# Weight scales found by way of DRAM instead of TensorE, and paced spreading of keys and queries, in a two-branch attention kernel

## The chip, the cores and the metric

The kernel runs on one core of a Trainium2 chip. The metric is the device time of one execution in microseconds. Three executions of the kernel before took 2800.7, 2800.9 and 2802.06 us; the median is 2800.9 us.

## The reference

Two attention blocks A and B read the same input `x` (2048 tokens, 640 features) and have weights of their own; a gate mixes their outputs.

```python
def _A_ref(x, wqkv, wo):                       # _B_ref is the same with its own weights
    H = 32; Dh = D // H                        # 32 heads of 20 features
    qkv = (x @ wqkv).reshape(B, S, 3, H, Dh)   # then q, k, v by head
    scores = einsum("bhqd,bhkd->bhqk", q, k) * Dh ** -0.5
    p = softmax(scores, axis=-1)
    o = einsum("bhqk,bhkd->bhqd", p, v)
    return o.transpose(0, 2, 1, 3).reshape(B, S, D) @ wo
g = sigmoid((x * gate_w).sum(-1, keepdims=True))
return g * a + (1 - g) * b
```

All inputs and the output are float32.

## The kernel before, in words

**Groups, units, steps.** The 64 heads of both blocks are 16 groups of four. A group has four blocks of 512 queries, and each of these has eight steps of 256 keys, so there are 512 steps. In a step TensorE makes eight products of keys and queries (`scores`, L639), ScalarE takes the exponential of each (L642), and two *value products* (`values`, L657; eight TensorE passes each) add the weighted values of the step before. Up to 15 steps ahead of a query block, TensorE makes the scores a second time the other way round (`max_mm`, L581), and VectorE finds their row maxima (L589, L592; for some of them ScalarE makes a helper with L585). Seven PSUM banks go round between the three engines (`take` and `give`).

**Block work.** Projections of the next group (`project_a`, `project_r`, `project_v`) and output products (`out_tiles`) are cut into blocks, and a step takes up to two of them (`slot`; their matmuls have L382). An output tile first loads its attention output from DRAM (`o_in<-o_scr`, L699), then lets `OWAIT` = 20 turns pass, then asks for its products.

**Turns.** What is not a matmul is written as generators in the list `side`. `advance` lets each of them go one `yield` further, and it is called eight times a step: this is a *turn*. A `yield PRODUCT` parks a generator until a value product is due (`product`, just before `values`), so that its small full-height matmuls stand beside the value product.

**Scales.** All weights are split into two float16 parts after a division by a power of two. For it `scales` (L167) needs the largest absolute value over the 128 partitions: the partition maxima are transposed on TensorE (L173), reduced on VectorE (L177), turned into powers of two by four small VectorE operations (`powers`), put on a diagonal (L183), sent back to all partitions by two TensorE products with ones (L190), and copied from PSUM (L193). Apart from the start, this is done twelve times: for queries and keys three times (`scales_qk`), for values seven times (`scales_v`), and for the output weights twice (`scales_o`). The results feed GpSimd, which splits the weights (L312 to L315).

**Spreading.** `project_a` leaves a group's keys and queries feature by feature. `spread` and `spread_differences` copy them by DMA to the rows where `scores` and `max_mm` want them, one transfer after each `yield` of `rows` (L428, L430), on SyncE's queue (SP). A group has two halves: the first takes 22 transfers (four of them for key differences), the second 18. Both halves wait until the group before has begun (`later`, L490), and then they go side by side. SP's queue is in order: it also issues the weights' loads (L240, L343, L344, L366), the row maxima's way through DRAM (L613, L617), the attention outputs' stores (L763), and the loads and stores of the output tiles (L699, L704, L732).

**What sets the order.** The program order of each engine is made by the loop over `G` (L1112) with the strings `STEP`; within an engine nothing is reordered when it runs. `clock`, `spend` and `tick_block` are the planner's own estimates, which choose PSUM banks.

Of the kernel before, what the change touches and what calls it, by code (L numbers as in the profile page):

```python
# [3 lines left out]

# [7 lines left out]
F32 = mybir.dt.float32  # L12
I32 = mybir.dt.int32
AF = mybir.ActivationFunctionType
OP = mybir.AluOpType
AX = mybir.AxisListType
# [3 lines left out]
P = 128  # L20
# [18 lines left out]
QUARTERS = (0, 128, 256, 384, 512)  # L39
FINE = (2, 3, 5, 6)  # L40
OB = 3
OWAIT = 20
AFROM, ADUE, ADUES = -24, -8, 4
QKMAX = (0, 10, 42, 10)
VEARLY = 338
# [23 lines left out]
def kernel(  # L69
# [10 lines left out]
    nc = tc.nc  # L80
# [5 lines left out]
    wts = ctx.enter_context(tc.tile_pool(name="wts", bufs=2))  # L86
    dram = ctx.enter_context(tc.tile_pool(name="dram", bufs=1, space=DRAM))
# [30 lines left out]
    o_scr = [dram.tile([2, D, S], F16, name=f"o_scr{z}") for z in range(2)]  # L118
    m_scr = [dram.tile([4, 16, P], F16, name=f"m_scr{i}") for i in range(2)]
    y_scr = dram.tile([NT, P, D], F32, name="y_scr")  # L120


    clock = {"pe": 0.0, "done": 0.0, "act": 0.0, "dve": 0.0}
# [11 lines left out]
    def spend(engine, cost, ready=0.0):  # L135

        clock[engine] = max(clock[engine], ready) + cost
        return clock[engine] + T_BACK
# [28 lines left out]
    def scales(maxima, n, then):  # L167

        for _ in range(REST):
            yield  # L170
        yield PRODUCT
        i, pt = take()
        nc.tensor.transpose(pt[:n, :P], maxima[:, :n], ident)  # L173
        tick_block(0.1, free_at[i])
        yield
        e = wts.tile([5, 8], F32, name="e", tag="scl", bufs=2)
        nc.vector.tensor_reduce(e[:n, 0:1], pt[:n, :P], axis=AX.X, op=OP.max)  # L177
        give(i, spend("dve", 0.3, clock["done"]))
        spend("dve", 1.0)
        powers(e.bitcast(I32)[:n, :], 1)  # L180
        dg = wts.tile([5, 2, 5], F32, name="dg", tag="scd", bufs=2)
        for k in range(2):
            nc.vector.tensor_scalar(dg[:n, k, :n], ident[:n, :n], e[:n, 3 + k:4 + k], None, op0=OP.mult)  # L183
        for _ in range(REST):
            yield
        yield PRODUCT
        i, pb = take()
        tick_block(0.1, free_at[i])
        for k in range(2):
            nc.tensor.matmul(pb[:, k * n:(k + 1) * n], ones[:n, :], dg[:n, k, :n], start=True, stop=True)  # L190
        yield
        both = wts.tile([P, 10], F32, name="both", tag="scb", bufs=2)
        nc.vector.tensor_copy(both[:, :2 * n], pb[:, :2 * n])  # L193
        give(i, spend("dve", 0.2, clock["done"]))
        then(both[:, :n], both[:, n:2 * n])

    def set_x(r_x, r, inv):
        nc.vector.tensor_copy(r_x, r)
        nc.vector.tensor_copy(inv_x, inv)

    def set_qk(i, r, inv):
        nc.vector.tensor_copy(r_qk[i], r)
        e = esc[i]
        nc.vector.tensor_tensor(e, inv[:, 0:1], inv_x, op=OP.mult)
        nc.vector.tensor_scalar(e, e, inv[:, 1:2], float(DH ** -0.5 / QKS ** 2), op0=OP.mult, op1=OP.mult)
        nc.vector.tensor_tensor(e, e, inv_x, op=OP.mult)

    def set_v(gg, r, inv):
        nc.vector.tensor_copy(r_v[gg], r)

        f = gg % (NG // 2) * 160
        while f < (gg % (NG // 2) + 1) * 160:
            p0 = f % P
            n = min(P - p0, (gg % (NG // 2) + 1) * 160 - f, (P, 32, 64, 32)[p0 // 32])
            nc.vector.tensor_copy(wrow[gg // (NG // 2)][p0:p0 + n, f // P:f // P + 1], inv[p0:p0 + n])
            f += n

    def scales_qk(i, maxima):

        return scales(maxima, 2, lambda r, inv: set_qk(i, r, inv))  # L220

    def scales_v(gg, maxima):
        return scales(maxima, 1, lambda r, inv: set_v(gg, r, inv))

    def scales_o(z, maxima):
        def then(r, inv):
            nc.vector.tensor_copy(r_o[z], r)
            nc.vector.tensor_scalar(f_o[z], gates[:, z, :], inv, inv_x, op0=OP.mult, op1=OP.mult)
            nc.vector.tensor_scalar(f_o[z], f_o[z], 1.0 / QKS, None, op0=OP.mult)

        return scales(maxima, 1, then)

    def largest(dst, src):
        nc.vector.tensor_reduce(dst, src, axis=AX.XY, op=OP.max,
# [46 lines left out]
    side = []  # L281
# [43 lines left out]
    spread_done = set()  # L325
# [107 lines left out]
    def spread(g, hl, t0, n, q=(0, 1), k=(0, 1), queues=repeat(nc.sync)):  # L433


        cols = slice(t0, t0 + n)
        r0 = 32 * (g % 4)
        qt = QT[g % 2]
        for j in range(2):
            base = 64 * j  # L440
            for pair in k:
                f = slice((2 * pair + j) * DH, (2 * pair + j + 1) * DH)
                yield from rows(KT[g % 2][:, pair, cols], base, 0, hl[f], DH, True, queues)
            if 0 in q:
                f = slice(GF + j * DH, GF + (j + 1) * DH)
                yield from rows(qt[:, 0, cols], base, 0, hl[f], DH, False, queues)
            if 1 in q:
                if j == 0:
                    yield from rows(qt[:, 1, cols], base, 0, hl[GF + 40:P], 8, False, queues)
                f = slice(r0 + 12 * j, r0 + 12 + 20 * j)  # L450
                yield from rows(qt[:, 1, cols], base, 8 * (1 - j), rk[g // 4][f, :, cols], 12 + 8 * j, False, queues)

    def project_r(i, ch):
        n = slice(ch * QB, (ch + 1) * QB)
        yield from project_chunk(blk["r", i], rk[i][:, 0, n], rk[i][:, 1, n], ch, QUARTERS if 4 * i in FINE else THIRDS)
        r_done.add((i, ch))
# [17 lines left out]
    def spread_differences(g, queues=repeat(nc.sync), to=None):  # L474
        dd = differences.pop(g)
        for j in range(2 if g == 0 else 1):
            for pair in range(2):
                f = slice((2 * pair + j) * DH, (2 * pair + j + 1) * DH)
                yield from rows((KD[g % 2] if to is None else to)[:, pair], 64 * j, 0, dd[f], DH, True, queues)

    def project_a(g, ch):
        if ch % 2 == 0:
            half_tiles(g)
        hl = blk["q", g]
        n = slice((ch % 2) * QB, (ch % 2 + 1) * QB)
        yield from project_chunk(blk["a", g], hl[:, 0, n], hl[:, 1, n], ch, QUARTERS if g in FINE else THIRDS)
        if ch == 1:
            key_differences(g, hl, work.tile([P, QB], F32, name="fs"), work.tile([P, 2, QB], F16, name="dd", bufs=1))
        if ch % 2 == 1:
            def later():  # L490
                for _ in range(10):
                    yield
                while not {(g // 4, c) for c in (ch - 1, ch)} <= r_done or now[0] < (g - 1) * NQ * NS + 1:
                    yield
                if ch == 1:
                    yield from spread_differences(g)
                yield from spread(g, hl, ch // 2 * 1024, 1024)
                spread_done.add((g, ch // 2))

            side.append(later())  # L500
# [383 lines left out]
    load, split_next = weights_a(1)  # L884
# [4 lines left out]
    r, inv = found  # L889
# [89 lines left out]
    def at(G, f):  # L979
        todo.setdefault(G, []).append(f)  # L980
# [11 lines left out]
    for g in range(2 * NG):  # L992
        b = g * step
        n = g + 1
        if n < 2 * NG:
            parts = 4 if n in FINE else 3
            fill += [((-8, 15)[g] if g < 2 else b + AFROM, b + ADUE + ADUES * ch if g else 4 + 3 * ch, parts, project_a(n, ch))
                     for ch in range(4)]
            if n + 1 < 2 * NG:
                tasks(b + 2 if g else 9, 3, weights_a(n + 1))  # L1000
            i = g // 4 + 1
            if i < 4:
                if g % 4 == 0:
                    z, c0 = i // 2, 320 * (i % 2)
                    srcs = max_tasks([[(wqkv[z], part * D + c0 + 160 * k) for k in range(2)] for part in range(2)],
                                     lambda m, i=i: scales_qk(i, m))
                    tasks(b + QKMAX[i], 2, srcs)
                if g % 4 == 2:
                    tasks(b + 6, 3, weights_r(i))
                    parts = 4 if 4 * i in FINE else 3  # L1010
                    fill += [(b + 12, b + 22 + 4 * ch, parts, project_r(i, ch)) for ch in range(4)]
            gg = g // 2 + 1
            if gg < NG and g % 2 == 0:
                load, scale, split = weights_v(gg)
                at(max(b - 8, 0), load)
                if gg < NG - 1:
                    at(max(b - 5, 3), lambda scale=scale: side.append(scale()))
                at(max(b - 1, 7), split)
                fill += [(max(b + 2, 10), b + 2 * step - 4 + j // 2, 2, project_v(gg, j)) for j in range(0, NT, 2)]
    early = weights_v(NG - 1)  # L1020
    at(VEARLY, early[0])
# [164 lines left out]
```

## Time and profile before

| | before |
|---|---|
| median of three executions | 2800.9 us |
| the profiled execution | 2800.33 us |
| its span (first to last instruction) | 2798.5 us |
| mean granted TensorE clock | 0.995 |
| TensorE (PE) busy | 2744.9 us |
| ScalarE (ACT) busy | 2524.6 us |
| VectorE (DVE) busy | 2452.3 us |
| GpSimd (POOL) busy | 671.9 us |

The span lies within the profiled execution, so 1.8 us of it are outside. The first value product starts at 105.6 us and the last pass of one at 2781.3 us: the 512 steps take 2675.7 us, 5.23 us each on average, and a turn is an eighth of it, 0.653 us. PEld is TensorE's weight load. A row of the timeline has its start, its length, engine, line, operation, output and inputs, how many instructions are merged into it, and in brackets the idle time ahead of it with what ended it. A row of the stretches' view has the stretch, its length, the busy time of PE, PEld, DVE, ACT and POOL (with counts), then TensorE's granted clock, the mean busy share of the 16 DMA engines, and GB/s. "SPq" is the time in which SP issues a DMA, not the transfer.

### The profile page before, as it was taken

What the parts mean: (1) busy time and instruction counts of PE and PEld (TensorE: products, weight loads), DVE (VectorE), ACT (ScalarE), POOL (GpSimd) and SP (SyncE); (2) the same over time, 40 slices, a digit from 0 to 9 for tenths busy, and PEclk for the clock granted to TensorE, in tenths of its full rate; (3) what the DMA queues carried; (4) which work ended last, traced back from release to release, by engine and by line L of the source; (5) the groups of instructions that cost most, each with busy time, mean ns of one, the idle gap of its engine ahead of it and who ended that gap; (6) DMA issues with size and microseconds to landing.
All of it is one profiled execution on the core that took longest, in us unless ns stands there. A gap on an engine that the chain in (4) does not pass through costs nothing.

```text
span 2798.5 us, 61863 instructions
## 1 busy us (share of the span) xinstructions
PE 2744.9 (98%) x23122; PEld 939.9 (34%) x23122; DVE 2452.3 (88%) x4795; ACT 2524.6 (90%) x5106; POOL 671.9 (24%) x914
## 2 busy tenths in 40 slices
PE   6999999999999999999999999999999999999998
PEld 3433332333333332333333323333333333322222
DVE  6789899889999999888888988989988898999982
ACT  3799999999999999999999889999999999989987
POOL 5322122312222421321221212222342202200111
PEclk9999999999999999999999999999999999999999
DMA  4020102001020211202012231122201112131112
GB/s 136 19 57 14 41 11 46 7 21 25 14 64 17 62 27 54 48 8 61 21 35 70 58 77 31 38 63 54 61 23 42 33 46 63 31 88 55 42 48 75
DMA packets 172943, 124.57 MB, mean 45 GB/s; under 512 B 103264, under 2 KB 142488, under 8 KB 172640
## 3 DMA queue, kind: packets, MB, share of 16 engines
q1 hardware_dynamic: 170096, 118.99, 16.9%
q8 instruction: 181, 2.97, 0.4%
q0 software_dynamic: 1600, 0.96, 0.2%
q14 instruction: 122, 1.00, 0.1%
q10 hardware_dynamic: 944, 0.66, 0.1%
HBM read 54.54 MB, written 31.85 MB: 31 GB/s over the span
## 4 chain that ended last, share of the span: by engine, by line
PE 92%; DVE 3%; ACT 2%; DMA 1%; POOL 1%; issue 1%; SPq 0%; POOLq 0%; ACTq 0%; DVEq 0%
PE acc L657 35%; PE bank L581 19%; PE bank L382 19%; PE bank L639 18%; DVE mpart L592 2%; ACT pt L642 1%; DMA xs<-in_A_x_dram 0%; ACT rl L585 0%; DMA wv<-in_A_wqkv_dram 0%; PE bank L820 0%; DVE rl L589 0%; PE bank L190 0%; SPq L428 0%; DVE ot L743 0%; PE bank L869 0%
## 5 line engine op out<-in xcount | busy, mean ns | idle before, releaser
L642 ACT ACTIVATE pt<-bank 128x512 f32<-128x512 f32 x4096 | 2169.2, 612 | 166.7 <-PE bank L639 101.7
L592 DVE TENSOR_REDUCE mpart<-bank 128x1 f32<-128x512 f32 x2976 | 1865.2, 682 | 222.2 <-PE bank L581 114.8
L657 PE MATMUL acc<-pt,v 128*21 128x512 f32 x8192 | 1082.2, 600 | 0.6 <-DVE ot L743 0.4
L639 PE MATMUL bank<-qt,kt 64*128 64x512 f16 x4096 | 1051.7, 380 | 4.2 <-ACT pt L642 2.0
L581 PE MATMUL bank<-kt,qt 60*128 60x512 f16 x3536 | 1021.3, 380 | 5.1 <-ACT pt L642 1.7
L581 PEld LDWEIGHTS <-qt 60*128 60x128 f16 x4096 | 238.1, 94 | 862.9 <-issue 802.9
L589 DVE CUSTOM_DVE_ANT_0 rl<-bank,rl 128x512 f32<-128x512 f32 x560 | 378.7, 680 | 16.7 <-ACT rl L585 10.6
L585 ACT ACTIVATE rl<-bank 128x512 f32<-128x512 f32 x560 | 329.7, 595 | 10.7 <-PE bank L581 8.7
L639 PEld LDWEIGHTS <-kt 64*128 64x128 f16 x4096 | 235.5, 94 | 238.7 <-issue 122.8
L382 PE MATMUL bank<-xx,wbh 128*128 128x168 f16 (+3 forms) x2400 | 286.0, 239 | 2.6 <-ACT xx L873 1.9
L657 PEld LDWEIGHTS acc<-pt,v 128*21 128x21 f32 x8192 | 143.1, 99 | 428.8 <-issue 421.9
L382 PE MATMUL bank<-xx,wbl 128*128 128x168 f16 (+3 forms) x1200 | 256.1, 237 | 0.0
L751 POOL TENSOR_TENSOR ot<-ot,sq 128x512 f32<-128x512 f32 x63 | 66.0, 1047 | 773.4 <-DVE sq L748 773.4
L382 PEld LDWEIGHTS <-wbh 128*128 128x128 f16 x2400 | 189.4, 98 | 109.5 <-issue 102.0
L581 PE MATMUL bank<-kd,qt 60*128 60x512 f16 x560 | 203.8, 380 | 1.6 <-DMA kd<-dd 1.2
L382 PE MATMUL bank<-woh,o_in 128*128 128x320 f16 (+1 forms) x640 | 156.4, 302 | 5.5 <-DMA o_in<-o_scr 5.4
L411 POOL CAST cq<-fs 128x512 f16<-128x512 f32 x60 | 36.6, 610 | 521.0 <-ACT fs L409 517.4
L382 PE MATMUL bank<-wvh,xx 128*128 128x160 f16 (+1 forms) x1280 | 155.2, 234 | 0.1
L382 PEld LDWEIGHTS <-xx 128*128 128x128 f16 x1920 | 131.5, 97 | 52.3 <-issue 49.1
L382 PE MATMUL bank<-wvl,xx 128*128 128x160 f16 (+1 forms) x640 | 137.3, 231 | 0.5 <-POOL wvl L322 0.5
L382 PEld LDWEIGHTS <-wbl 128*128 128x128 f16 x1200 | 117.4, 98 | 4.3 <-issue 0.8
L382 PEld LDWEIGHTS <-o_in 128*128 128x128 f16 (+1 forms) x960 | 80.9, 97 | 97.7 <-issue 63.8
(131 smaller groups left out, 1259.1 us busy)
## 6 DMA issues: line engine op xcount, KB each, us to landing
y_scr<-y_out SPq DMA_DIRECT2D x48, 320.0 KB
y_out<-y_scr SPq DMA_DIRECT2D x32, 320.0 KB
kt<-cq SPq DMA_DIRECT2D x120, 80.0 KB
o_scr<-on SPq DMA_DIRECT2D x240, 40.0 KB
o_in<-o_scr SPq DMA_DIRECT2D x64, 96.0 KB
kt<-cq SPq DMA_DIRECT2D x136, 40.0 KB
wstage<-in_B_wqkv_dram SPq DMA_DIRECT2D x13, 400.0 KB
xs<-in_A_x_dram SPq DMA_DIRECT2D x8, 640.0 KB
```

The costliest lines, as they stand in the source:

```text
L382: nc.tensor.matmul(out_ap, a, b, start=(k == 0), stop=(k == len(pairs) - 1))
L411: nc.gpsimd.tensor_copy(hi, f)
L581: nc.tensor.matmul(pt, QT[g % 2][r, pair, q0:q0 + P], k, start=True, stop=True)
L585: nc.scalar.activation(relus[u, j], pt, AF.Relu)
L589: nc.vector.tensor_tensor_reduce(rl, pt, rl, 1.0, LOW, OP.add, OP.max, m)
L592: nc.vector.tensor_reduce(m, pt, axis=AX.X, op=OP.max)
L639: nc.tensor.matmul(et, KT[g % 2][r, pair, kt * P:(kt + 1) * P], QT[g % 2][r, pair, qb * QB:(qb + 1) * QB], start=True, stop=True)
L642: nc.scalar.activation(pt, et, AF.Exp, scale=factor(g // 4))
L657: nc.tensor.matmul(acc[32 * h:32 * h + VW, :], V[(g // 2) % 2][:, kt, (g % 2) * GH + h, :], ptiles.pop((G, kk, h)), start=(kt == 0), stop= ...
L751: nc.gpsimd.tensor_tensor(t3, t3, sq.unsqueeze(2).to_broadcast([P, 16, 32]), op=OP.mult)
```

## The change

`scales_qk`, `scales_v` and `scales_o` call a new function, `scales_by_dram`. The partition maxima are stored to DRAM; ten turns later one transfer loads them into every partition (128 x 128 values, or 128 x 128 pairs for queries and keys); 18 turns after that VectorE takes the maximum in every partition at once and goes on with `powers`. No TensorE instruction is left in it, and nothing waits for a value product. The start still uses `scales`. The values' weights are loaded and reduced one step earlier. `paced` puts a further `yield` behind each transfer of a spread (`PACE` = 2; group 1 keeps its old rate), and the second half of a group waits for the first. As the code stands, a transfer comes every second turn. `OWAIT` goes from 20 to 24.

```diff
-OWAIT = 20
+STORED, LOADED = 10, 18
+OWAIT = 24
+PACE = 2
...
+    s_scr = [dram.tile([P * 5], F32, name=f"s_scr{i}") for i in range(3)]
+    scale_turns = counter()
...
+    def scales_by_dram(maxima, n, then):
+
+        turn = next(scale_turns)
+        scr = s_scr[turn % 3].rearrange("(p n) -> p n", n=5)[:, :n]
+        yield
+        yield
+        nc.sync.dma_start(scr, maxima[:, :n])
+        for _ in range(STORED):
+            yield
+        rows = wts.tile([P, P, 2], F32, name="srows", tag="srows", bufs=2)[:, :, :n]
+        nc.sync.dma_start(rows, scr.unsqueeze(0).to_broadcast([P, P, n]))
+        for _ in range(LOADED):
+            yield
+        e = wts.tile([P, 10], F32, name="es", tag="ses", bufs=2)
+        nc.vector.tensor_reduce(e[:, :n], rows.rearrange("p q n -> p n q"), axis=AX.X, op=OP.max)
+        spend("dve", 0.35 * n + 0.5)
+        powers(e.bitcast(I32), n)
+        then(e[:, 3 * n:4 * n], e[:, 4 * n:5 * n])
...
-        return scales(maxima, 2, lambda r, inv: set_qk(i, r, inv))
+        return scales_by_dram(maxima, 2, lambda r, inv: set_qk(i, r, inv))
...
-        return scales(maxima, 1, lambda r, inv: set_v(gg, r, inv))
+        return scales_by_dram(maxima, 1, lambda r, inv: set_v(gg, r, inv))
...
-        return scales(maxima, 1, then)
+        return scales_by_dram(maxima, 1, then)
...
+    def paced(gen, n):
+        for _ in gen:
+            for _ in range(n):
+                yield
...
                 while not {(g // 4, c) for c in (ch - 1, ch)} <= r_done or now[0] < (g - 1) * NQ * NS + 1:
                     yield
+                while ch == 3 and (g, 0) not in spread_done:
+                    yield
+                turns_each = 1 if g == 1 else PACE
                 if ch == 1:
-                    yield from spread_differences(g)
-                yield from spread(g, hl, ch // 2 * 1024, 1024)
+                    yield from paced(spread_differences(g), turns_each)
+                yield from paced(spread(g, hl, ch // 2 * 1024, 1024), turns_each)
                 spread_done.add((g, ch // 2))
...
-                at(max(b - 8, 0), load)
+                at(max(b - 9, 0), load)
                 if gg < NG - 1:
-                    at(max(b - 5, 3), lambda scale=scale: side.append(scale()))
-                at(max(b - 1, 7), split)
+                    at(max(b - 6, 3), lambda scale=scale: side.append(scale()))
+                at(max(b - 1, 8), split)
```

**First place: TensorE at the fifth scale of the values.** Before, the scale's transpose stands ahead of one value product (L657), between scores (L639), maxima (L581) and the matmuls of a block (L382):

```order
L639 MATMUL bank_93<-qt_81,kt_83 128x512
L173 MATMUL bank_89<-ident,m_18933 1x128
L657 MATMUL acc<-pt,v_87 21x512 x4
L581 LDWEIGHTS qt_80
L581 MATMUL bank_94<-kt_82,qt_80 128x512
```

One step further on, the two products with ones stand ahead of the next first value product:

```order
L639 MATMUL bank_92<-qt_81,kt_83 128x512
L190 MATMUL bank_91<-dg,ones 128x1 x2
L657 MATMUL acc<-pt,v_87 21x512 x4
L581 LDWEIGHTS qt_80
L581 MATMUL bank_90<-kt_82,qt_80 128x512
```

Now, with the lines moved by 31, the value product (L688) follows the scores (L670) directly; L612 are the maxima:

```order
L670 MATMUL bank_92<-qt_81,kt_83 128x512
L688 MATMUL acc<-pt,v_87 21x512 x4
L612 LDWEIGHTS qt_80
L612 MATMUL bank_94<-kt_82,qt_80 128x512
```

Three TensorE instructions are gone from each of the twelve scales, one that stood ahead of one value product and two ahead of another, and two PSUM banks fewer are taken each time.

**Second place: SP's queue where the second scale of queries and keys and the fourth of the values come together.** In the program of after, the store of the pair's maxima (L207), the row maxima's way (L644, L648), an output tile's store (L763), the two loads (L211) and the next output tile's loads (L730) stand in this order:

```order
L207 DMA s_scr_128<-m_14307 128x2
L207 DMA s_scr_126<-m_14309 128x1
L644 DMA m_scr_123<-m4r 16x4x32 x4
L648 DMA qt_80<-m_scr_123 4x512 x4
L763 DMA y_scr<-y_out 128x640
L211 DMA srows<-s_scr_128 128x128x2
L211 DMA srows<-s_scr_126 128x128x1
L730 DMA o_in<-o_scr_121 128x3x128 x2
```

The two big loads are neighbours in one queue, behind a store that waits for an output product, and VectorE's two reductions of them (L215) stand nine instructions apart.

**Third place: SP's queue in the spread of group 10.** Before, the load of output tile 6 of the second job (L699) stands behind nearly all of both halves' transfers (L428, L430); these are the rows just ahead of it:

```order
L430 DMA kt_82<-cq 20x1024
L430 DMA qt_80<-rk 20x1024
L613 DMA m_scr_124<-m4r 16x4x32 x4
L428 DMA qt_80<-cq 40x1x1024
L430 DMA qt_80<-cq 20x1024
L428 DMA qt_80<-rk 40x1x1024
L699 DMA o_in<-o_scr_121 128x2x128 x2
L704 DMA y_out<-y_scr 128x640
```

Now the same load (L730) comes where the first half is not yet half done (L451, L453):

```order
L451 DMA qt_80<-cq 40x1x1024
L644 DMA m_scr_124<-m4r 16x4x32 x4
L453 DMA qt_80<-cq 20x1024
L451 DMA qt_80<-cq 16x1x1024
L730 DMA o_in<-o_scr_121 128x2x128 x2
L735 DMA y_out<-y_scr 128x640
L453 DMA qt_80<-cq 8x1024
```

The same output products of that tile follow four steps after its turn in both programs; what changed is how many transfers SP has to issue ahead of its load.

More of the change, by code (lines that the diff above doesn't have):

```diff
@@ L2 @@
 from contextlib import ExitStack
-from itertools import cycle, repeat
+from itertools import count as counter, cycle, repeat
 import concourse.bass as bass
```

## The prediction

> **What bounds the kernel now.** I read the page's busy times first, then the chain that ended last.
>
> ```profile
> PE 2744.9 (98%) x23122; PEld 939.9 (34%) x23122; DVE 2452.3 (88%) x4795; ACT 2524.6 (90%) x5106; POOL 671.9 (24%) x914
> ```
> ```profile
> PE 92%; DVE 3%; ACT 2%; DMA 1%; POOL 1%; issue 1%; SPq 0%; POOLq 0%; ACTq 0%; DVEq 0%
> ```
>
> TensorE is busy 98% of the span and owns 92% of the chain. Time taken from it should come off the end, unless VectorE or ScalarE, at 88% and 90% on average, is full at that very place. TensorE's timeline shows one scale at close range; these are its value products (L657) and the scale's own rows.
>
> ```profile
> 1907.62 1.06 PE L657 MATMUL acc<-pt,v 128*21 128x512 f32 x8
> ...
> 1909.36 0.27 PE L173 MATMUL bank<-ident,m 128*1 128x128 f32 x1
> 1909.56 1.06 PE L657 MATMUL acc<-pt,v 128*21 128x512 f32 x8
> ...
> 1913.06 1.05 PE L657 MATMUL acc<-pt,v 128*21 128x512 f32 x8
> ...
> 1915.22 0.60 PE L190 MATMUL bank<-dg,ones 1*128 1x1 f32 x4 [0.26 <-ACT pt L642]
> 1915.75 1.06 PE L657 MATMUL acc<-pt,v 128*21 128x512 f32 x8
> ...
> 1919.39 1.06 PE L657 MATMUL acc<-pt,v 128*21 128x512 f32 x8
> ...
> 1921.14 1.06 PE L657 MATMUL acc<-pt,v 128*21 128x512 f32 x8
> ```
>
> The distance between value products is a ruler. From 1919.39 to 1921.14 it is 1.75 us, the plain short distance. With the transpose it is 1.94, with the two products 2.69 (1913.06 to 1915.75); 0.26 of that is a wait for a PSUM bank. The long distance, with a block of projections in it, is 3.50 ahead of the products and 3.64 behind them.
>
> **Part 1: twelve scales leave TensorE.** One scale costs 0.19 + 0.94 us here, and up to 0.14 in the block behind it; I take 1.2 us. Their number:
>
> ```profile
> L173 PE MATMUL bank<-ident,m x12: 270/270/271, 128.1 to 1999.5; 128*1 128x128 f32 x9, 128*2 128x128 f32 x3
> ```
>
> Twelve times 1.2 is **14.4 us**, and 15.2 with the whole 0.14. The lower bound comes from VectorE, which is nearly full where no block runs:
>
> ```profile
> 420.00:440.00 20.00, 19.76 (x139) 4.63 (x138) 19.44 (x45) 17.94 (x37) 8.34 (x7) 1.00 0.05 12
> 748.00:766.00 18.00, 17.46 (x117) 4.23 (x110) 17.62 (x41) 15.48 (x31) 4.63 (x4) 1.00 0.07 14
> ...
> 1077.00:1099.00 22.00, 21.28 (x154) 6.38 (x152) 20.76 (x55) 18.51 (x38) 5.30 (x5) 1.00 0.16 42
> ```
>
> It idles 0.6, 0.4 and 1.2 us in these stretches, which hold four scales. If TensorE's 4.8 us come back only that far, 12 us are left of the 14.4. VectorE's own work hardly moves: a reduction over 128 values gives way to another, `powers` stays, three tiny operations go.
>
> **Part 2: the spread stops blocking SP.** One stall stands alone in the trace.
>
> ```profile
> 1644.38 1.06 PE L657 MATMUL acc<-pt,v 128*21 128x512 f32 x8
> ...
> 1647.58 1.06 PE L657 MATMUL acc<-pt,v 128*21 128x512 f32 x8
> ...
> 1649.33 1.06 PE L657 MATMUL acc<-pt,v 128*21 128x512 f32 x8
> ...
> 1656.32 0.45 PE L382 MATMUL bank<-woh,o_in 128*128 128x320 f16 x1 [5.39 <-DMA o_in<-o_scr]
> ...
> 1659.42 1.47 PE L657 MATMUL acc<-pt,v 128*21 128x512 f32 x8
> ...
> 1661.58 0.63 PE L657 MATMUL acc<-pt,v 128*21 128x512 f32 x4
> ```
>
> From 1649.33 to 1659.42 are 10.09 us where the same kind of distance before (1644.38 to 1647.58) is 3.20, and the short one behind is 2.16 instead of 1.75: together **7.3 us**. TensorE waited for `o_in`, which SP issued at 1654.24, late because every transfer of the spread holds SP 0.8 us while two halves hand it one each per turn of 0.65 us:
>
> ```profile
> 1654.24 0.92 SPq L699 DMA_DIRECT2D o_in<-o_scr  x2
> ```
> ```profile
> L428 SPq DMA_DIRECT2D kt<-cq x136: 762/797/1121, 40.5 to 2491.1; - x136
> ```
>
> Now one half comes at a time, a transfer every second turn: SP needs 0.8 of 1.3 us and keeps up, and this load is issued four steps, 21 us, ahead of its use. The price of pacing: a group's last transfer goes out some 9 steps after the group before has begun, instead of 2. The maxima that read it start 17 steps after that beginning at the earliest (15 steps ahead of the group's own), so 8 steps (42 us) cover it, and I cost it at nothing; without that cover every later step would wait. `OWAIT` shifts products by half a step within dues of several steps: nothing, with at most one block's delay either way.
>
> **Part 3: the new wait.** VectorE now waits for a DMA, and behind it in its queue stand all maxima and so the PSUM banks. The load writes 128 x 128 values separately (the tile has two columns, the DRAM rows five), 16384 pieces of 4 or 8 bytes. No row shows such a load alone. The nearest are the four loads of L366, together 4 x 5 x 128 = 2560 pieces of 128 bytes, and a store of L613, 16 x 4 = 64 pieces of 64 bytes, each in a stretch of its own:
>
> ```profile
> 480.52:483.04 2.52, 2.52 (x23) 0.56 (x20) 2.08 (x5) 2.26 (x6) 0.00 (x0) 1.00 0.86 130
> 500.67:500.86 0.19, 0.19 (x5) 0.19 (x4) 0.19 (x1) 0.19 (x2) 0.00 (x0) 1.00 0.23 21
> ```
> ```profile
> q1 hardware_dynamic: 170096, 118.99, 16.9%
> ```
> ```profile
> kd<-dd POOLq DMA_DIRECT2D x8, 20.0 KB, 2.0
> ```
>
> Share times length times 16 engines over pieces gives 0.86 x 2.52 x 16 / 2560 = 13.5 ns for 128 bytes and 10.9 ns for 64. The straight line through both gives an estimate of 8.5 ns at 4 bytes, my value. An engine has 1024 pieces: 8.7 us, and with the 2.0 us that a small transfer takes to land, 10.7. The upper end is the queue's mean packet, 0.169 x 16 x 2798.5 us / 170096 = 44.5 ns (of 700 bytes): 47.6 us.
>
> How long may it take? The reduction comes 18 turns behind the load:
>
> ```profile
> L657 PE MATMUL acc<-pt,v x8192: 592/600/1026, 105.6 to 2781.3; 128*21 128x512 f32 x200
> ```
>
> 2675.7 us over 512 steps of eight turns is 0.653 us a turn, so 11.8 us. SP is often ahead of its turn: it may load as soon as the store has landed, 17 us ahead of the reduction. I take 14.5 in the middle. A load that lands in 10.7 us costs nothing at either end.
>
> The pair is different: two loads, one behind the other, in one queue.
>
> ```profile
> 1075.84 0.15 DVE L276 TENSOR_REDUCE m<-wmax 128x2 f32<-128x8 f32 x1
> ```
> ```profile
> 1084.69 0.35 SPq L732 DMA_DIRECT2D y_scr<-y_out  x1
> ```
>
> The maxima are ready at 1075.8, and the reductions come 30 turns later, at 1095.4. SP cannot load before the output store at 1084.69, so from 1085.0 on; the second load lands 2 + 2 x 8.7 = 19.4 us later, at 1104.4. VectorE waits 9.0 us. TensorE goes on for about 0.9 until its seven banks are taken and loses 0.4 restarting, as above: **8.5 us**. Its lower end is nothing, if SP gets the loads out early.
>
> [...] The 500.67 stretch moved 64 pieces in 0.19 us, 3.0 ns each over all engines. [...]
>
> **The sum.** 2800.33 (the profiled execution: span 2798.5 and 1.8 around it) - 14.4 - 7.3 + 8.5 = 2787.1; the median of the runs lies 0.6 above that execution, so **2787.7 us**.
>
> **The rivals.**
> - *The loads land late* (slower). All ten single loads stall VectorE, and with it TensorE, once a piece costs over 12.2 ns, (14.5 - 2) / 1.024. The gains of 21.7 us are used up at 12.7 ns. At the 13.5 ns of the 128-byte row each single wait is 1.3 us and the pair's 18.7: 13 + 18.7 - 21.7 = +10, 2811 us. At 44.5 ns it would be about 3190. For it: all engines read the same few DRAM rows, which no row here shows. Against it: the price falls with size in both rows.
> - *Pieces go one after another.* 16384 x 8.5 ns = 139 us a load; ten waits of 127 and one of 269: about 4320 us. Against it: 2560 pieces went in 2.52 us. [...]
> - *VectorE paces, or the tile's load stays late* (same). If part 1 gives only 6 us, 2796; if the early `o_in` is caught behind something else and the 7.3 stay, 2795.
> - *The pair doesn't wait*: 2779.
>
> **How the numbers follow.** Forecast 0.55; no wait in the pair 0.15; same 0.13; loads late 0.16; one after another 0.01. A run of this kernel can tell 0.2%, 5.6 us, from no change: faster means below 2795.3. So faster 0.70, same 0.13, slower 0.17. The range takes in the pair without a wait and the cases of no change, 2776 to 2803; the late loads beyond stay out.
>
> **What would show it.** Right: no matmul of the scales behind the start; distances of 1.75 where 1.94 and 2.69 stood; no distance of 10 us near 1650; VectorE waiting for `srows` once, near 1095, for 9 us, and landing of a single load within 11 us of its issue. Wrong: waits for `srows` at ten or twelve places, or TensorE waiting for `qt` or `kt` in maxima (L612), which would be the pacing.

## The result and the profile after

The changed kernel takes **2850.2 us** (median of five runs, 2849.3 to 2853.2) beside 2802.1 us for the kernel before (2800.7 to 2802.3, five runs). The ratio is 1.0176, with a 95% interval of 1.0165 to 1.0186: slower by 48 us. The forecast was 2787.7, faster, with a range that ended at 2803. The rival "the loads land late" is what came.

The profile page after has the line of busy times, the two lines of the chain, and DMA's packets and first queue:

```profile
PE 2748.1 (96%) x23062; PEld 935.2 (33%) x23062; DVE 2450.0 (86%) x4759; ACT 2524.3 (89%) x5106; POOL 672.9 (24%) x914
...
DMA packets 371469, 125.54 MB, mean 44 GB/s; under 512 B 301792, under 2 KB 341016, under 8 KB 371168
...
q1 hardware_dynamic: 368624, 119.99, 20.4%
...
PE 83%; DMA 8%; DVE 4%; ACT 2%; SPq 1%; issue 1%; POOL 1%; POOLq 0%; DVEq 0%; ACTq 0%
```

TensorE lost its 60 instructions of the scales (23122 to 23062) and yet is busy 3.2 us longer. DMA went from 1% of the chain to 8%. The queue has 198528 more packets; twelve loads of 16384 pieces make 196608 of them. One line of the waits' view names the new wait, and two name TensorE behind it (total, times, longest):

```profile
DVE es L215 <- DMA srows<-s_scr: 52.9, 11, 14.6
...
PE bank L670 <- DVE mpart L623: 39.7, 18, 20.0
...
PE bank L612 <- DVE mpart L620: 15.5, 5, 3.8
```

VectorE waits for the load at eleven of twelve scales, not at one. The timeline shows a single load of after, from SP's issue to the reduction that waited for it:

```profile
425.92 0.38 SPq L211 DMA_DIRECT2D srows<-s_scr  x1
...
443.66 0.29 DVE L215 TENSOR_REDUCE es<-srows 128x1 f32<-128x128 f32 x1 [6.00 <-DMA srows<-s_scr]
```

17.7 us lie between the two, where 10.7 had been forecast; the other eight single loads that were waited for took 17.7 to 18.3. This is the pair:

```profile
1100.84 16.71 SPq L211 DMA_DIRECT2D srows<-s_scr  x2
...
1118.88 0.42 DVE L215 TENSOR_REDUCE es<-srows 128x2 f32<-128x256 f32 x1 [5.09 <-DMA srows<-s_scr]
...
1135.19 0.28 DVE L215 TENSOR_REDUCE es<-srows 128x1 f32<-128x128 f32 x1 [14.58 <-DMA srows<-s_scr]
```

The second load lands 16.3 us behind the first, so the pieces of one load take 16.3 us, 1.0 ns each, and what lies around them is the rest, some 1.5 us (1.4 to 2.0). One engine of the sixteen spends 15.9 ns a piece, on the mean (16.3 us x 16 / 16384). The stretches' view (TensorE's granted clock, then the DMA share, stand third and second from the end) shows that the engines were not busy with that:

```profile
1103.00:1119.00 16.00, 13.76 (x103) 3.22 (x98) 9.48 (x18) 13.83 (x28) 0.00 (x0) 1.00 0.57 10
1119.00:1135.00 16.00, 0.00 (x0) 0.00 (x0) 1.44 (x9) 0.00 (x0) 0.00 (x0) 0.57 0.59 11
1135.00:1140.00 5.00, 3.01 (x14) 0.42 (x15) 4.70 (x16) 1.19 (x2) 3.52 (x3) 0.50 0.64 167
```

A share of 0.57 times 15.9 ns is 9 ns, and the trace's packet records of these pieces last 8.9 ns on the mean: a piece itself is nearly as cheap as forecast, and for the other 7 ns, on the mean, an engine has no packet on record. In the second row TensorE and ScalarE stand still for 16 us, and VectorE nearly so. How TensorE comes out of a wait is seen behind the single load shown above:

```profile
436.07 1.06 PE L688 MATMUL acc<-pt,v 128*21 128x512 f32 x8
...
439.41 1.06 PE L688 MATMUL acc<-pt,v 128*21 128x512 f32 x8
...
445.69 0.58 PE L670 MATMUL bank<-qt,kt 64*128 64x512 f16 x1 [5.22 <-DVE mpart L623]
...
447.42 1.77 PE L688 MATMUL acc<-pt,v 128*21 128x512 f32 x8
...
451.06 1.06 PE L688 MATMUL acc<-pt,v 128*21 128x512 f32 x8
```

439.41 to 447.42 is 8.01 us where 1.75 would stand, and the next distance is 3.64 where 2.85 stood before: 7.0 us for one wait of 6.00. A score takes 0.58 us instead of 0.38 and a value product 1.77 instead of 1.06, while the granted clock is down to 0.50:

```profile
437.00:444.00 7.00, 3.21 (x22) 0.82 (x19) 0.97 (x4) 3.45 (x7) 0.00 (x0) 0.86 0.64 23
444.00:448.00 4.00, 2.31 (x10) 0.52 (x13) 3.89 (x14) 1.62 (x3) 3.13 (x2) 0.50 0.18 39
448.00:456.00 8.00, 7.88 (x54) 1.72 (x50) 7.14 (x14) 6.47 (x14) 1.67 (x1) 0.94 0.37 83
```

The granted clock is 0.50 for the 4 us behind the wait. Read microsecond by microsecond, the clock is 1.00 up to 442 and 0.50 from 443 to 448: it fell about 1.6 us after TensorE had stopped at 440.47. It is 1.00 again from 449 on, some 3.3 us after the restart at 445.69. Around a wait of 1.87 us it fell as well: the clock is 0.50 from 1480 to 1483, and the next value product takes 1.91 us:

```profile
1478.96 0.37 PE L612 MATMUL bank<-kt,qt 60*128 60x512 f16 x1 [1.87 <-DVE mpart L620]
...
1480.67 1.91 PE L688 MATMUL acc<-pt,v 128*21 128x512 f32 x8
```

The two gains, on the other hand, are there. These are value products of after at the place of the old stall near 1650:

```profile
1693.77 1.06 PE L688 MATMUL acc<-pt,v 128*21 128x512 f32 x8
1695.52 1.06 PE L688 MATMUL acc<-pt,v 128*21 128x512 f32 x8
...
1698.72 1.06 PE L688 MATMUL acc<-pt,v 128*21 128x512 f32 x8
1700.47 1.06 PE L688 MATMUL acc<-pt,v 128*21 128x512 f32 x8
```

1695.52 to 1698.72 is 3.20 us where 10.09 stood, and 1.75 follows where 2.16 stood.

So the theory was open at one point: why 16384 pieces, cheap as they are, take 16 us. Either the number of pieces sets the time, at a price that I had too low; or, as the rival had it, it is that all engines read the same few DRAM rows. All 128 partitions read the same 2560 bytes.

### The profile page after: what moved, and what is told of

Read it like the earlier page. It is cut to its first block, busy times and chain, and to the rows that moved or that the text cites. A ratio compares the mean times of both kernels' runs of the same rounds, so it can differ in the third digit from the quotient of the medians.

```text
span 2850.1 us, 61802 instructions
## 1 busy us (share of the span) xinstructions
PE 2748.1 (96%) x23062; PEld 935.2 (33%) x23062; DVE 2450.0 (86%) x4759; ACT 2524.3 (89%) x5106; POOL 672.9 (24%) x914
## 3 DMA queue, kind: packets, MB, share of 16 engines
q1 hardware_dynamic: 368624, 119.99, 20.4%
## 4 chain that ended last, share of the span: by engine, by line
PE 83%; DMA 8%; DVE 4%; ACT 2%; SPq 1%; issue 1%; POOL 1%; POOLq 0%; DVEq 0%; ACTq 0%
PE acc L688 31%; PE bank L405 18%; PE bank L612 17%; PE bank L670 16%; DMA srows<-s_scr 7%; DVE mpart L623 2%; ACT pt L673 1%; DMA xs<-in_A_x_dram 0%; DVE rl L620 0%; ACT rl L616 0%; PE bank L851 0%; SPq L644 0%; DMA wv<-in_A_wqkv_dram 0%; DMA m_scr<-m4r 0%; SPq L648 0%
## 5 line engine op out<-in xcount | busy, mean ns | idle before, releaser
L670 PE MATMUL bank<-qt,kt 64*128 64x512 f16 x4096 | 1058.2, 382 | 43.0 <-DVE mpart L623 39.7
L688 PE MATMUL acc<-pt,v 128*21 128x512 f32 x8192 | 1090.1, 604 | 1.7 <-DVE ot L774 1.6
L612 PE MATMUL bank<-kt,qt 60*128 60x512 f16 x3536 | 1024.4, 382 | 12.6 <-DVE mpart L620 8.0
L612 PEld LDWEIGHTS <-qt 60*128 60x128 f16 x4096 | 238.5, 94 | 910.6 <-issue 851.5
L620 DVE CUSTOM_DVE_ANT_0 rl<-bank,rl 128x512 f32<-128x512 f32 x560 | 377.1, 677 | 16.5 <-ACT rl L616 11.3
L616 ACT ACTIVATE rl<-bank 128x512 f32<-128x512 f32 x560 | 329.8, 595 | 25.0 <-PE bank L612 15.9
L670 PEld LDWEIGHTS <-kt 64*128 64x128 f16 x4096 | 236.4, 95 | 251.0 <-issue 135.0
L688 PEld LDWEIGHTS acc<-pt,v 128*21 128x21 f32 x8192 | 143.3, 99 | 444.7 <-issue 437.3
L612 PE MATMUL bank<-kd,qt 60*128 60x512 f16 x560 | 204.2, 381 | 9.3 <-DVE mpart L620 7.5
```

The source lines that it names most:

```text
L612: nc.tensor.matmul(pt, QT[g % 2][r, pair, q0:q0 + P], k, start=True, stop=True)
L616: nc.scalar.activation(relus[u, j], pt, AF.Relu)
L620: nc.vector.tensor_tensor_reduce(rl, pt, rl, 1.0, LOW, OP.add, OP.max, m)
L670: nc.tensor.matmul(et, KT[g % 2][r, pair, kt * P:(kt + 1) * P], QT[g % 2][r, pair, qb * QB:(qb + 1) * QB], start=True, stop=True)
L688: nc.tensor.matmul(acc[32 * h:32 * h + VW, :], V[(g // 2) % 2][:, kt, (g % 2) * GH + h, :], ptiles.pop((G, kk, h)), start=(kt == 0), stop= ...
```

## The experiments

**Whole rows.** The maxima are packed in DRAM, and a partition reads them as one run of 512 or 1024 bytes: 128 pieces a load. By the pages, the first queue has 195072 packets fewer than in the changed kernel (173552 against 368624), 12 x 16256.

```diff
-        scr = s_scr[turn % 3].rearrange("(p n) -> p n", n=5)[:, :n]
+        flat = s_scr[turn % 3][:P * n]
+        scr = flat.rearrange("(p n) -> p n", n=n)
...
-        nc.sync.dma_start(rows, scr.unsqueeze(0).to_broadcast([P, P, n]))
+        nc.sync.dma_start(rows, flat.unsqueeze(0).to_broadcast([P, P * n]))
...
```

> The kernel of after with the maxima packed in DRAM and loaded into every partition as one whole run of 512 bytes (1024 for queries and keys): 128 pieces a load instead of 16384. Theory (the loss is the landing of 16384 separate pieces, about 1 ns each over all engines): a load lands within 3 us, VectorE has no wait for srows, and both gains stand: 2802.1 - 14.4 - 7.3 = about 2780 us. Rival (the loss lies in the way through DRAM itself, in the store, the wait of SP for it and the neighbours it delays): the time stays above 2830 us.

Measured: **2784.9 us** (2783.7 to 2785.5), ratio to before 0.9940 (0.9926 to 0.9953). No reduction waits; the load that took 17.7 us above is there within 5.9:

```profile
427.54 0.35 SPq L212 DMA_DIRECT2D srows<-s_scr  x1
...
433.40 0.28 DVE L216 TENSOR_REDUCE es<-srows 128x1 f32<-128x128 f32 x1
```

The wait for the load is the whole loss, 65.3 us from this kernel to the changed one. Its two parts can be read: TensorE waits 50.0 us longer for VectorE's maxima (39.7 + 15.5 against 3.9 + 1.3, from the waits' view of the two), and its same 23062 matmuls are busy 16.7 us longer (2748.1 against 2731.4), at the lower clock behind each wait (0.985 on the mean of the execution, 0.996 with whole rows). Together they are 66.7 us. The kernel is also faster than before, though by 5 us less than expected; that comes back below.

**Half the pieces from a packed stretch.** The same packed source, while the destination has a gap behind every two values (for queries and keys, every two pairs): 8192 pieces of 8 or 16 bytes, from 512 bytes for a scale of the values and the output, and from 1024 for queries and keys. By the pages, the first queue has 96768 packets more than with whole rows (270320 against 173552), 12 x 8064. The edit is against the whole-row kernel; the reduction is adapted to the gaps.

```diff
-        rows = wts.tile([P, 2 * P], F32, name="srows", tag="srows", bufs=2)[:, :P * n]
-        nc.sync.dma_start(rows, flat.unsqueeze(0).to_broadcast([P, P * n]))
+        rows = wts.tile([P, P // 2, 2 * 2 + 1], F32, name="srows", tag="srows", bufs=2)[:, :, :2 * n]
+        nc.sync.dma_start(rows, flat.rearrange("(q k) -> q k", k=2 * n).unsqueeze(0).to_broadcast([P, P // 2, 2 * n]))
...
```

> The kernel of after with the maxima packed in DRAM and a gap in the tile behind every second value (pair), so that a load has 8192 pieces of 8 (16) bytes. Theory (time by number of pieces, about 1 ns each): a load takes half as long, 8 us and about 2 us to land; the ten single loads cause no wait, the second of the pair about 8 us; total about 2802.1 - 21.7 + 8 = 2788 us. Rival (a load has a cost that does not go with the number, or goes with what lies behind it in the queue): single waits of 2 to 4 us stay, and the total is above 2815 us.

Measured: **3135.8 us** (3131.8 to 3140.0), ratio 1.1192 (1.1177 to 1.1207). Half as many pieces took more than twice as long. A load of values:

```profile
467.35 0.38 SPq L212 DMA_DIRECT2D srows<-s_scr  x1
...
508.91 0.29 DVE L216 TENSOR_REDUCE es<-srows 128x1 f32<-128x128 f32 x1 [36.28 <-DMA srows<-s_scr]
```

and a load of queries and keys, with as many pieces, from twice the bytes:

```profile
288.90 0.38 SPq L212 DMA_DIRECT2D srows<-s_scr  x1
...
309.93 0.43 DVE L216 TENSOR_REDUCE es<-srows 128x2 f32<-128x256 f32 x1 [7.82 <-DMA srows<-s_scr]
```

41.6 us and 21.0 us. The theory that the number of pieces sets the time has fallen: the same number took twice as long from half the bytes. In the stretch of the load of values the engines are busy only 0.12 of the time:

```profile
470.00:508.00 38.00, 5.17 (x36) 1.17 (x33) 2.49 (x5) 5.42 (x11) 0.00 (x0) 0.61 0.12 8
```

**Own rows.** 16384 pieces as in the changed kernel, but each partition reads a row of its own of the input. The scales then come from `x` and not from the weights, so this kernel serves for its time alone; its loads also need not wait for the store of the maxima, which the wide rows below do again.

```diff
-        nc.sync.dma_start(rows, scr.unsqueeze(0).to_broadcast([P, P, n]))
+        nc.sync.dma_start(rows, x_t[:, 0, :].rearrange("p (q n) -> p q n", n=5)[:, :, :n])
```

> The kernel of after, but every partition loads its 128 values from a row of the input x of its own (2560 bytes a partition, every fifth value) instead of all of them from the same row of scratch; the scales then come from x and not from the weights. Theory (number of pieces): as after, 16 us a load, 17.7 us from issue to the reduction, total about 2850 us. Rival (all engines read the same few rows of DRAM and stand in line there): a load takes 9 to 11 us, no single wait, total about 2790 us.

Measured: **2793.1 us** (one run), 57 below the changed kernel with the same pieces. Only the pair waits:

```profile
1077.09 10.79 SPq L211 DMA_DIRECT2D srows<-in_A_x_dram  x2
...
1089.95 0.41 DVE L215 TENSOR_REDUCE es<-srows 128x2 f32<-128x256 f32 x1
...
1099.19 0.29 DVE L215 TENSOR_REDUCE es<-srows 128x1 f32<-128x128 f32 x1 [7.51 <-DMA srows<-in_A_x_dram]
```

SP was let go at 1087.9 and the second load was there at 1099.2, 11.3 us later: about 9.8 us of pieces with the same 1.5 around them, 9.6 ns a piece and engine. This is near what the prediction had for the price.

From these three a size law could be read off before the next runs: time of a piece times the bytes that the pieces lie in is constant. With 1.5 us taken off each landing, 8192 pieces from 512 bytes took 40.1 us, 4.89 ns each, and 4.89 x 512 = 2500; from 1024 bytes 19.5 us, 2.38 ns, 2440; and in the changed kernel, from 2560 bytes, 0.99 ns, 2540.

**Wider rows.** The changed kernel with one number changed: the same pieces from 5120 bytes.

```diff
-    s_scr = [dram.tile([P * 5], F32, name=f"s_scr{i}") for i in range(3)]
+    s_scr = [dram.tile([P * 10], F32, name=f"s_scr{i}") for i in range(3)]
...
-        scr = s_scr[turn % 3].rearrange("(p n) -> p n", n=5)[:, :n]
+        scr = s_scr[turn % 3].rearrange("(p n) -> p n", n=10)[:, :n]
```

> The changed kernel with one number changed: a partition's row in DRAM is 10 values long instead of 5, so the 16384 pieces of a load come from 5120 bytes instead of 2560. Theory (reads of one small stretch of DRAM queue up; time = 2500 byte-ns per piece over the bytes that the pieces lie in, as 41 us for 8192 pieces from 512 bytes, 20 for 8192 from 1024 and 16.0 for 16384 from 2560 gave): 8.0 us by the stretch, so the pieces' own 9.3 us decide, as where every partition read its own row: no single load waits, the second of the pair some 7 us, 2793 us. Rival (time by number of pieces): 2850 as the changed kernel.

Measured: **2793.6 us** (2792.7 to 2794.6), ratio 0.9971 (0.9960 to 0.9982). With all partitions still reading the same values in as many pieces into the same tile, one number in the layout turns the change from slower into faster. The load that took 17.7 us takes 12.1, and the wait of 6.00 is 0.25:

```profile
420.29 0.38 SPq L211 DMA_DIRECT2D srows<-s_scr  x1
...
432.41 0.28 DVE L215 TENSOR_REDUCE es<-srows 128x1 f32<-128x128 f32 x1 [0.25 <-DMA srows<-s_scr]
```

In its stretch the engines are busy 0.92 of the time, where they were busy 0.57 in the changed kernel:

```profile
420.30:430.00 9.70, 9.64 (x70) 2.33 (x68) 9.26 (x18) 9.52 (x20) 1.78 (x2) 1.00 0.92 9
```

**Narrower rows.** The same number the other way, 3 in place of 5: the same pieces from 1536 bytes.

> The changed kernel with the same number changed the other way: a partition's row is 3 values long, the 16384 pieces come from 1536 bytes. Theory (as for the rows of 10): 16384 x 2500 / 1536 = 26.7 us for the pieces of a load, 28.2 with the 1.5 us around them, 10.5 more than the 17.7 of the changed kernel; nine single loads 10.5 later, the pair's second 21, the first some 4: about 2850 + 120 = 2970 us. Rival (number of pieces): 2850.

Measured: **2985.6 us** (one run), 15 us above what the law gave. The single load:

```profile
448.89 0.38 SPq L211 DMA_DIRECT2D srows<-s_scr  x1
...
477.42 0.29 DVE L215 TENSOR_REDUCE es<-srows 128x1 f32<-128x128 f32 x1 [17.07 <-DMA srows<-s_scr]
```

28.5 us, where the law said 28.2. In all, four widths obey it (2440 to 2540), and at the fifth, 5120 bytes, the pieces' own price takes over: 10.6 us, where the law gives 8.0. How far apart neighbouring pieces lie does not give this order by itself: time times that distance is 38 to 39 byte-ns for the packed pieces, 8 and 16 bytes apart, and 20 for those 12 and 20 bytes apart.

**Pacing alone.** The kernel before, its scales on TensorE, with `paced`, the wait for the first half and `OWAIT` of 24.

```diff
-OWAIT = 20
+OWAIT = 24
+PACE = 2
...
+                while ch == 3 and (g, 0) not in spread_done:
+                    yield
+                turns_each = 1 if g == 1 else PACE
                 if ch == 1:
-                    yield from spread_differences(g)
-                yield from spread(g, hl, ch // 2 * 1024, 1024)
+                    yield from paced(spread_differences(g), turns_each)
+                yield from paced(spread(g, hl, ch // 2 * 1024, 1024), turns_each)
```

> The kernel before with the pacing of the spread, the order of its halves and OWAIT 24, and with the scales on TensorE as before. Theory (the 10 us distance near 1650 us came from SP, which the two halves had filled): that distance becomes 3.2 us, total 2802.1 - 7.3 = about 2795 us, ratio 0.9974. Rival (the early end of the spread was needed somewhere): no gain or a loss, TensorE waiting in the maxima.

Measured: **2795.4 us** (2794.8 to 2796.1), ratio 0.9978 (0.9969 to 0.9987), 6.4 us for Part 2. The distance at the stall is 3.21:

```profile
1650.20 1.06 PE L666 MATMUL acc<-pt,v 128*21 128x512 f32 x8
...
1653.41 1.06 PE L666 MATMUL acc<-pt,v 128*21 128x512 f32 x8
```

**Scales alone.** Whole rows, without the pacing and with `OWAIT` of 20: what is left is that twelve scales are off TensorE.

```diff
-OWAIT = 24
+OWAIT = 20
...
-                while ch == 3 and (g, 0) not in spread_done:
-                    yield
...
-                    yield from paced(spread_differences(g), turns_each)
-                yield from paced(spread(g, hl, ch // 2 * 1024, 1024), turns_each)
+                    yield from spread_differences(g)
+                yield from spread(g, hl, ch // 2 * 1024, 1024)
```

> The change without its Part 2 (no pacing, OWAIT 20 again), and with the whole-row load that lands without a wait: what is left is the twelve scales gone from TensorE alone. Theory (VectorE gives part of it back): the paced whole-row kernel moved its last value product forward by 15.9 us, 7.3 of them at the stall near 1650, so 8.6 are left for the scales: 2802 - 8.6 = 2793.4 us, the distance of 10 us near 1650 there again. Rival (the prediction's Part 1, 14.4 us): 2787.6.

Measured: **2791.3 us** (2789.8 to 2793.4), ratio 0.9966 (0.9954 to 0.9978). Part 1 is worth 10.2 us of 2801.6, between the 8.6 that I expected and the prediction's 14.4. The stall is there again, 10.51 us from value product to value product:

```profile
1640.62 1.06 PE L687 MATMUL acc<-pt,v 128*21 128x512 f32 x8
...
1648.11 0.45 PE L406 MATMUL bank<-woh,o_in 128*128 128x320 f16 x1 [5.89 <-DMA o_in<-o_scr]
...
1651.13 1.06 PE L687 MATMUL acc<-pt,v 128*21 128x512 f32 x8
```

The parts add up: 6.4 of pacing and 10.2 of scales make 16.6, and the whole-row kernel, which has both, gained 16.9.

**The scale's work in three.** What is missing from Part 1? In the whole-row kernel VectorE does a scale in one go, here 1.6 us between two groups of maxima:

```profile
1997.22 0.69 DVE L624 TENSOR_REDUCE mpart<-bank 128x1 f32<-128x512 f32 x1
1997.83 0.28 DVE L216 TENSOR_REDUCE es<-srows 128x1 f32<-128x128 f32 x1
...
1999.21 0.23 DVE L253 TENSOR_SCALAR f_o<-f_o 128x16 f32<-128x16 f32 x1
1999.29 1.88 DVE L624 TENSOR_REDUCE mpart<-bank 128x1 f32<-128x512 f32 x3
```

and TensorE waits 0.70 us for the maximum behind it:

```profile
2000.03 0.37 PE L671 MATMUL bank<-qt,kt 64*128 64x512 f16 x1 [0.70 <-DVE mpart L624]
2000.33 1.06 PE L689 MATMUL acc<-pt,v 128*21 128x512 f32 x8
```

In the kernel before, the trip to TensorE and back had parted this work in two. The edit cuts it in three, three turns apart, with the load's turns shortened by as many.

```diff
-STORED, LOADED = 10, 18
+STORED, LOADED = 10, 12
...
-        spend("dve", 0.35 * n + 0.5)
+        spend("dve", 0.35 * n + 0.1)
+        for _ in range(3):
+            yield
         powers(e.bitcast(I32), n)
+        spend("dve", 0.3)
+        for _ in range(3):
+            yield
         then(e[:, 3 * n:4 * n], e[:, 4 * n:5 * n])
```

> The whole-row load, paced, with a scale's VectorE work (reduction, powers, copies: about 1.4 us in one go) cut into three, three turns apart, and the load's turns cut from 18 to 12 so that a scale is ready when it was. Theory: the one go holds a PSUM bank back, so TensorE waits 0.4 to 1.1 us behind each scale, and that is what is missing from Part 1 (14.4 - 8.6 = 5.8 us): cut in three, most of it comes back, about 2781 us. Rival: VectorE is full around the scales whatever the order: 2785 as with whole rows.

Measured: **2781.6 us** (2780.7 to 2782.8), ratio 0.9929 (0.9916 to 0.9943). It is the fastest version here. Against the whole-row kernel it is 3.3 us less; the two intervals overlap, but the times of the two do not, and in the profiles the last value product stands 2.9 us earlier (against before, 18.8 us instead of 15.9). Part 1 had fallen short by 4.2 us by the times (14.4 less 10.2) and by 5.8 by the distances (14.4 less 8.6), so this edit brought back half of it or more. How it does so is shown in part: TensorE's waits for maxima fall from 5.2 us (3.9 + 1.3) to 3.6 (3.0 + 0.6), and the rest of the gain is not located. The edit also brings the reduction forward by six turns, which was not tried apart from the cut. Some of what is still missing can be seen: at the last scale TensorE waits 0.84 us. The rows are VectorE's multiplication of the gates, and TensorE's score that waits for the maxima behind it.

```profile
1995.51 0.88 DVE L257 TENSOR_SCALAR f_o<-gates,es,inv_x 128x16 f32<-128x16 f32 x1
```

```profile
1997.25 0.39 PE L676 MATMUL bank<-qt,kt 64*128 64x512 f16 x2 [0.84 <-DVE mpart L629]
```

## Why the prediction was wrong, point by point

- **The step that failed is Part 3's price of a piece**, "the straight line through both gives an estimate of 8.5 ns at 4 bytes", and so "10.7" us of landing. It measured 15.9 ns and 17.7 us. How VectorE comes to wait was worked out nearly rightly: with 15.9 ns in place of 8.5, the prediction's own sum gives each single load a wait of 3.8 us (2 + 1.024 x 15.9 - 14.5), and the nine that came were 3.7 on average; it gives the pair 24 us, and 19.7 came (5.1 + 14.6). Part 3 as a whole, 8.5 us in the sum, measured 65.3. Both rows behind the line came from transfers whose pieces lie far apart; the load's lie in 2560 bytes, and there the stretch sets the time: 16.3 us a load from 2560 bytes, 10.6 from 5120. The prediction named this ("all engines read the same few DRAM rows, which no row here shows") but gave it no price of its own, only a share in a rival of 0.16.
- **The 8.5 ns by itself** was not far from what an unhindered piece costs: from own rows and from rows of 10 values, a load took 9.8 and 10.6 us of pieces, 11.3 and 12.1 with what lies around them. That the straight line came so near was in part luck. By the trace's packet records the stretch of its 64-byte row holds 16 packets of 4 bytes besides, and the 64-byte pieces took 9.3 ns and not 10.9; a line through 9.3 and 13.4 gives some 5.5 at 4 bytes.
- **The break-even held as far as it was tried.** It stood at 12.7 ns; 15.9 ns gave a slower kernel and 9.6 ns a faster one, and nothing between was run. With a price near the forecast the pair cost 8.7 us (2793.6 with wide rows against 2784.9 with whole rows), and 8.5 had been forecast. That agreement is in part luck: with wide rows the loads went out 6.1 us behind the maxima (1070.54 to 1076.62) instead of 9.2, and the second landed 22.6 us later instead of 19.4.
- **The price of a wait was too low.** "TensorE goes on for about 0.9 ... and loses 0.4 restarting" left out the clock: of the 65.3 us that the waits cost, 16.7 are TensorE's own work at a lower clock (a mean of 0.985 against 0.996). With waits of 52.9 us alone the time would have come out at some 2838.
- **Part 1 was too large**: 14.4 forecast, its lower end 12, and 10.2 measured. The instructions left as counted (TensorE 13.5 us less busy in the whole-row kernel, 2744.9 to 2731.4), but VectorE gave part of it back, as the rival "VectorE paces" had it. That rival had VectorE's idle time as its reason; the last run, which moves the same work into three places, brought back half of that part or more, so the order of the work on VectorE was as much of a reason.
- **Part 2 was right**: 7.3 forecast at the stall, 3.20 for 10.09 in its place, and 6.4 in time, with the interval of its ratio reaching from 3.6 to 8.7 us. The costs at nothing held: in the pacing-alone kernel TensorE has no new wait for `qt` or `kt`.
- **The number of pieces was right**: of the 198528 packets that the queue has more, twelve loads of 16384 make 196608. Such a load's pieces took some 10 to 27 us here, by their stretch.

With what the parts measured by themselves the sum is 2802.1 - 10.2 - 6.4 + 65.3 = 2850.8 us. The 65.3 is taken from the changed kernel itself; only the other terms are independent of it.

## What to carry to other kernels

Before a tiny result is sent to all partitions by way of DRAM, look at how many bytes the pieces are read from, and not only at how many pieces there are: pack it so that each partition reads one run, or else lay it out wide. Here a load of 16384 pieces took 17.7 us from 2560 bytes and 12.1 from 5120, and with one run of 512 bytes a partition it was there within 5.9. A price of a transfer is only worth what its nearest row shares with it, and where a text says "no row shows this", that case needs a price of its own and its end in the range. When work leaves the engine that sets the pace, ask also whether the engine that takes it over does it in one go, and cut the go where a buffer is waited for behind it; here TensorE waited 0.70 us behind one go, and the cut into three brought 3.3 us.

## What the runs showed of the hardware

- Loads of 8192 or 16384 small pieces from one narrow stretch of DRAM went at a rate that followed the stretch: 4.9 ns a piece from 512 bytes, 2.4 from 1024, 1.65 from 1536 and 1.0 from 2560, while the engines' share of busy time was down to 0.12 from 512 bytes and 0.57 from 2560. From 5120 bytes a piece took 0.65 ns and from own rows 0.60 (10.6 and 9.8 us a load). Whether it is the extent, the number of distinct blocks in it, or that the engines go through them in the same order was not tried and stays open.
- SP was held by the issue behind such a load: 16.2 us in the changed kernel's pair (10.3 with own rows), and 32.1 us by an ordinary store of 40 KB that came 0.4 us behind a load from 512 bytes:

```profile
467.77 32.12 SPq L795 DMA_DIRECT2D o_scr<-on  x1
```

- A wait of 5.2 us cost TensorE 7.0, some 2 us more than its length, with a granted clock of 0.50 for the 4 us behind it. All ten pauses of TensorE behind late loads, from 1.9 us up, were followed by a granted clock of 0.50.
